# The first pair of blocks: keys first, corner Gram products, and 32x32 turns on VectorE instead of two trips through DRAM

## The chip, the cores and the metric

The kernel runs on one core of a Trainium2 chip. A core has TensorE (PE; its weight loads are listed apart as PEld), VectorE (DVE), ScalarE (ACT), GpSimd (POOL) and SyncE (SP), each with an instruction queue of its own, and 16 DMA engines which the queues of SP, ACT and POOL feed. The metric is device time in microseconds of one execution, the median of several runs.

## The reference

A delta-rule attention over 4 sequences, 8 heads, 768 steps and heads of 48, followed by a two-layer network with a leaky ReLU (384 to 2048 to 384), all in float32.

```python
k_n = k / (np.linalg.norm(k, axis=-1, keepdims=True) + 1e-06)
for t in range(S):
    y[:, :, t] = einsum('bhd,bhde->bhe', q[:, :, t], state)
    v_old = einsum('bhde,bhd->bhe', state, kt)
    state = state + bt * einsum('bhd,bhe->bhde', kt, vt - v_old)
h = x @ w_in          # x: the y of all heads side by side
return np.maximum(0.01 * h, h) @ w_out
```

## The kernel before

The 768 steps are cut into 12 blocks of 64. Within a block the recurrence is solved in closed form: the Gram matrix of the block's keys, scaled by beta over the squared norm, gives a triangular 64x64 system for each of the 32 pairs of head and sequence, and its inverse T turns the loop into matrix products.

Each block passes through these steps, written as Python generators that a function `weave` interleaves in program order; the scheduler of the language then orders every engine's queue by its own estimate of time. `issue_after` (the helper `behind`) pins an instruction behind another one on its engine.

- `gram(n)`, L181: for each of two groups `g` (two sequences each) it loads keys and queries side by side (`kq`, L190), multiplies the keys with keys and queries in one product of 128 columns (`pg`, L207), copies the key half (`gs`, L211), stores its two 32x32 diagonal corners to DRAM (`gd`, L215), masks the query half with the strict triangle (`rq`, L222), keeps the lower-left corner (`gm`, L226), and at last loads the corners back as `L` (L230), one pair of head, sequence and half on each partition.
- `norms` (L237) takes the diagonal of `L`, makes the square root by a bit shift and two Newton steps on VectorE (L245 to L254), and the factor beta over the norm squared.
- `inv(b)`, L278: 31 elimination steps on VectorE (`eliminate`, L269 and L274) turn `L` into the inverse `T` of every 32x32 corner. Blocks 0 and 1 are handled together on 128 partitions, every later block alone on 128 partitions with half the width. The result leaves through DRAM: `td` (L314) and, after a transposing copy `Tt` on ACT (L306), `tt` (L315).
- `merge`, L319: loads `T` into the tile `t` (L325) and its transposed twin into `gm` (L327), both with the rows where TensorE wants them, and makes the lower-left corner of the full inverse with two sets of 32x32 products, `pz` (L341) and `pu` (L349); their copies `zs` (L343) and `rt` (L353, L355) are shared between ACT and VectorE.
- `solve(n)`, L361: loads keys, values and queries (L373, L374), scales the values (`rv`, L395), and makes `pk`, `pw`, `pc`, `py` (L390 to L421); `columns` (L442) transposes the result into the network's input (`px`, split into two parts `xh` and `xl`).
- `ffn(n)`, L455: for each of 16 slices `f` of the hidden width the first layer `ph` (L475), the activation on ACT (L479, L480), the rest `gl` on VectorE (L482), and two slices later the second layer `po` (L465). Weights come as float64 words that are decoded on the chip.
- `weights()`, L134: for each `f` the decoding, one ACT pass (L153) and four VectorE passes (L155, L159, L160, L161), then `low`, which makes the low part of both matrices with TensorE (`wl`, L142 to L144) and ACT (L145, L163). Three slices (KA) are decoded in the prologue; passes of the others are pinned behind the last elimination step of the first pair (`mark["inverse"]`). A weight load (L128) that starts late is gated by a two-column VectorE fill (L126).

The prologue runs gram(0) and gram(1) with three weights, the first inverse, and solve(0). Then, in each block's FFN, the solve of the next block, the inverse of the one after it and the Gram products of the third one ahead are woven in; in block 0's FFN also the remaining weights.

Of the kernel before, what the change touches and what calls it, by code (L numbers as in the profile page):

```python
# [9 lines left out]
F32 = mybir.dt.float32  # L10
# [39 lines left out]
def delta_moe_kernel(ctx: ExitStack, tc, kqT, kv, qT, beta, cst, w_all, out, nblk):  # L50
# [43 lines left out]

    def statics():
        nc.scalar.dma_start(csb, cst)
        for t in ring["t"]:
            nc.vector.memset(t, 0.0)
        for x in "vq":
            for t in ring[x]:  # L100
                nc.gpsimd.memset(t[0:R0], 0.0)

    def identities():
        for t in ring["k"]:
            nc.vector.tensor_copy(
# [15 lines left out]
    def load_w(f, gate=None):  # L121
        if f < NFC:
# [4 lines left out]
            with behind("L"):  # L127
# [6 lines left out]
    def weights():  # L134
# [12 lines left out]
        last = None  # L147
# [28 lines left out]
    def dq(n):  # L176

        return nc.scalar if n < 2 else nc.sync


    def gram(n):  # L181
        if n * NGR >= Q_BUFS:
            need(sv, solve, n - Q_BUFS // NGR)
        kqs = []
        for g in range(NGR):
            t = sb.tile([P, GS, NPAIR, 2, C], F32, tag="kq", name=f"kq{n}_{g}", bufs=KQ_BUFS)
            kqs.append(t)
            with behind("L"):
                for b in range(2):
                    (nc.sync, nc.scalar)[b if n < 2 else 0].dma_start(  # L190
                        t[b * R0:b * R0 + D].rearrange("p s u x t -> p (s u x t)"), kqT[n, g, b])
        b0, i = where[n]
        if i == 0:
            Lh[b0] = sb.tile([P, HC, HC], F32, tag="L", name=f"L{b0}", bufs=2)
        gd = dr.tile([64, HC, HC], F32, tag="gd", name=f"gd{n}")
        for g in range(NGR):
# [4 lines left out]
            ps = [(ps_o if n == 1 else ps_a).tile([P, 512], F32, tag=f"o{b}" if n == 1 else "a", name=f"pg{n}_{g}_{b}") for b in range(2)]  # L201
# [10 lines left out]
            for c in range(2):  # L212
                for e in range(2):
                    a = e * HS + g * GH + c * GU
                    (nc.sync, nc.scalar)[e if n < 2 else 0].dma_start(  # L215
# [12 lines left out]
            if g == NGR - 1:  # L228
                for r in (i,) if len(NB[b0]) > 1 else (0, 1):
                    d = nc.sync.dma_start(Lh[b0][r * 64:(r + 1) * 64].rearrange("l j i -> l (j i)"), gd.rearrange("l j i -> l (j i)"))  # L230
                if n == 1:
                    mark["L"] = d.ins
# [4 lines left out]
    def norms(n, n2):  # L237

        p, w = P, HC
        s, r, c, z = (sb.tile([P, wd], F32, tag=t, name=f"{t}{n}", bufs=b)  # L240
                      for t, wd, b in (("sr", HC, 1), ("rc", HC, 1), ("cb", HC, 2), ("sq", C, 2)))
        nrm[n] = z
        dq(2 * n).dma_start(c, beta[n])
# [15 lines left out]
    def eliminate(b, L, j, T, m):  # L259
# [13 lines left out]
        for tv, t in parts:  # L273
            i = nc.vector.tensor_tensor(t, t, tv, ALU.subtract)  # L274
        if b == 0:
            mark["inverse"] = i.ins

    def inv(b):  # L278

        for n in NB[b]:  # L280
            need(gg, gram, n)
# [4 lines left out]
        with behind("gl"):  # L286
# [319 lines left out]
```

## Time and profile before

| | us |
|---|---|
| median of 3 runs | 711.48 (709.86 to 712.53) |
| the profiled execution's own time | 711.66 |
| its span, first to last instruction | 709.9 |
| TensorE busy | 642.5 |
| VectorE busy | 465.2 |
| ScalarE busy | 332.5 |
| first FFN matmul (`ph`) starts | 93.80 |
| block 0's results are copied out (`ob`) | 174.5 |

The page gives, for each engine, the time it was busy and that share of the span, and cuts the span into 40 slices of some 17.7 us with the busy tenths of each engine in them. In a timeline row the first number is the start, the second the length; the bracket tells how long the engine had been idle before and what ended that. In the chain of waits each row is a piece of the one chain that ended last. Matmul ends are modelled, so starts are the surer numbers there.

### The profile page before, as it was taken

To read this page: it belongs to the slowest core of one execution; us is meant where nothing else is said; L and a number is where in the kernel's file an instruction comes from. 1 tells how busy PE (TensorE), PEld (TensorE's weight loads), DVE (VectorE), ACT (ScalarE), POOL (GpSimd) and SP (SyncE) were. 2 spreads that over 40 slices of the span, in tenths; PEclk is the share of its full clock that TensorE was granted. 3 is DMA by queue.
4 is the path that set the end of the run, shared out by engine and by line. 5 is a ranking of instruction groups with operands and counts; after the bars stand their busy time and mean duration, and the time that the engine had idled before them with its cause. 6 is when DMAs were issued, how large, how long until landed. Compare 5 with 4: busy or idle time off the path is not lost.

```text
span 709.9 us, 21034 instructions
## 1 busy us (share of the span) xinstructions
PE 642.5 (91%) x8424; PEld 591.8 (83%) x8424; DVE 465.2 (66%) x2053; ACT 332.5 (47%) x832; POOL 7.3 (1%) x12
## 2 busy tenths in 40 slices
PE   4800499999999999999999999999999999999996
PEld 3500487889999999999999999999999999999996
DVE  6589159995875975965956947858759759431221
ACT  3311364765463554554544544634635544545422
POOL 4000000000000000000000000000000000000000
PEclk9955599999999999999999999999999999999999
DMA  9295567105527137055065073172270340310001
GB/s 239 40 294 156 110 173 214 48 3 96 130 51 147 31 64 160 4 93 132 3 117 111 2 141 86 39 135 54 52 158 19 66 115 2 69 23 2 13 12 23
DMA packets 128481, 60.90 MB, mean 86 GB/s; under 512 B 115136, under 2 KB 118336, under 8 KB 128384
## 3 DMA queue, kind: packets, MB, share of 16 engines
q1 hardware_dynamic: 115072, 56.81, 35.4%
q10 hardware_dynamic: 13312, 2.76, 2.2%
q8 instruction: 66, 1.08, 0.7%
q14 instruction: 31, 0.25, 0.1%
HBM read 46.96 MB, written 12.58 MB: 84 GB/s over the span
## 4 chain that ended last, share of the span: by engine, by line
PE 81%; DVE 9%; DMA 5%; ACT 2%; issue 1%; ACTq 0%; SPq 0%; DVEq 0%
PE ph L475 29%; PE po L465 27%; PE pw L403 4%; PE pg L207 3%; PE py L421 3%; PE pk L390 3%; DVE rv L395 3%; PE wl L142 3%; PE pc L411 2%; PE pu L349 2%; PE px L450 2%; PE pz L341 2%; DVE tmp L269 1%; DVE T L274 1%; DMA cb<-in_beta 1%
## 5 line engine op out<-in xcount | busy, mean ns | idle before, releaser
L475 PE MATMUL ph<-xh,w 128*128 128x256 f32 x1152 | 248.2, 289 | 0.2 <-DVE gl L482 0.2
L475 PEld LDWEIGHTS ph<-xh,w 128*128 128x128 f32 x1152 | 190.8, 189 | 7.7 <-DVE gl L482 2.1
L465 PE MATMUL po<-w,gh 128*128 128x384 f32 x768 | 190.3, 340 | 2.7 <-ACT gh L479 2.7
L482 DVE TENSOR_TENSOR gl<-ph,gh 128x256 fp32r<-128x256 f32 x192 | 81.2, 424 | 138.5 <-ACT ph L480 128.9
L475 PE MATMUL ph<-xl,w 128*128 128x256 f32 x576 | 166.0, 289 | 0.9
L479 ACT ACTIVATE gh<-ph 128x256 fp32r<-128x256 f32 x192 | 73.9, 385 | 149.4 <-PE ph L475 147.2
L465 PEld LDWEIGHTS po<-w,gh 128*128 128x128 f32 x768 | 131.1, 189 | 4.6 <-ACT gh L479 4.5
L465 PE MATMUL po<-w,gl 128*128 128x384 f32 x384 | 119.5, 340 | 0.0
L274 DVE TENSOR_TENSOR T<-T,tmp 128x60 f32<-128x60 f32 (+35 forms) x661 | 113.0, 208 | 1.2
L269 DVE TENSOR_TENSOR tmp<-T,L 128x60 f32<-128x60 f32 (+35 forms) x661 | 113.0, 208 | 0.7
L475 PEld LDWEIGHTS ph<-xl,w 128*128 128x128 f32 x576 | 108.7, 189 | 4.2 <-DVE xl L119 2.7
L480 ACT ACTIVATE ph<-ph 128x256 f32<-128x256 f32 x192 | 73.4, 382 | 0.0
L465 PEld LDWEIGHTS po<-w,gl 128*128 128x128 f32 x384 | 68.1, 189 | 0.5
L222 DVE TENSOR_TENSOR rq<-pg,csb 64x256 f32<-64x256 f32 x96 | 40.6, 423 | 22.9 <-ACT gs L211 21.8
L341 PE MATMUL pz<-rt,gm 32*32 32x32 f32 x768 | 20.0, 196 | 38.6 <-DMA rt<-td 38.6
L341 PEld LDWEIGHTS pz<-rt,gm 32*32 32x32 f32 x768 | 16.1, 111 | 41.4 <-DMA rt<-td 38.7
L207 PE MATMUL pg<-kq 48*64 48x128 f32 x768 | 35.6, 295 | 5.7 <-DMA kq<-in_kqT 5.7
L207 PEld LDWEIGHTS pg<-kq 48*64 48x64 f32 x768 | 28.3, 144 | 14.7 <-DMA kq<-in_kqT 6.5
L119 DVE TENSOR_TENSOR xl<-px,xh 128x256 fp32r<-128x256 f32 x36 | 14.2, 422 | 29.5 <-ACT xh L118 29.1
L392 ACT ACTIVATE rt<-pk 48x512 f32<-48x512 f32 x44 | 26.1, 593 | 13.2 <-PE pk L390 12.4
L142 PE MATMUL wl<-cg,csb 128*128 128x384 f32 x64 | 28.3, 538 | 4.2 <-ACT gs L211 4.2
L405 ACT COPY rv<-pw 64x384 f32<-64x384 f32 x48 | 22.7, 472 | 18.1 <-PE pw L403 17.3
(67 smaller groups left out, 665.4 us busy)
## 6 DMA issues: line engine op xcount, KB each, us to landing
wr<-in_w_all SPq DMA_DIRECT2D x16, 768.0 KB, 6.7
kq<-in_kqT SPq DMA_DIRECT2D x44, 192.0 KB, 4.2
L<-gd SPq DMA_DIRECT2D x22, 256.0 KB, 3.8
rk<-in_kv SPq DMA_DIRECT2D x24, 192.0 KB, 3.2
rv<-in_kv SPq DMA_DIRECT2D x24, 192.0 KB, 4.2
rq<-in_qT SPq DMA_DIRECT2D x24, 192.0 KB, 3.9
out<-ob SPq DMA_DIRECT2D x48, 96.0 KB, 3.0
gd<-gs SPq DMA_DIRECT2D x88, 32.0 KB, 2.7
```

The lines of the kernel that those rows point to most:

```text
L142: nc.tensor.matmul(d, eye, g[:, cols], start=True, stop=False)
L207: nc.tensor.matmul(ps[b][c * 64:(c + 1) * 64, p * 128:(p + 1) * 128], kq[r, c ^ b, p, 0], kq[r, c ^ b, p].rearrange("p x t -> p (x t)"), s ...
L222: nc.vector.tensor_tensor(qa[DN, c, b * NPAIR:(b + 1) * NPAIR], pv[b][r, 1], tri[r].rearrange("p (o t) -> p o t", o=1).broadcast_to([C, NP ...
L269: nc.vector.tensor_tensor(tv, t[:, :, j:j + 1].broadcast_to([P, k, w]), L[:, j, j + 1:].rearrange("p (o w) -> p o w", o=1).broadcast_to([P ...
L274: i = nc.vector.tensor_tensor(t, t, tv, ALU.subtract)
L341: nc.tensor.matmul(zv[h * 64:h * 64 + HC, u], gt[lo, l], t[lo, h, u, HC:], start=True, stop=True)
L403: nc.tensor.matmul(pv[r, u], t[:, c, u], v[:, c, u], start=True, stop=True)
L465: i = nc.tensor.matmul(po[t][:, :DO], a[:, ts_], w[f], start=(f == 0 and k == 0), stop=(f == NFC - 1 and k == 2))
L475: nc.tensor.matmul(ph, a[f][:, cc * P:(cc + 1) * P], x[cc][e], start=(k == 0), stop=(k == 3 * NCC - 1))
L479: nc.scalar.activation(gh, ph, AF.Prelu, alpha=0.01)
L480: i = nc.scalar.activation(ph, ph, AF.Prelu, alpha=0.01)
L482: i = nc.vector.tensor_tensor(gl, ph, gh.bitcast(F32), ALU.subtract)
```

## The change

Only the first pair of blocks (0 and 1) and the prologue are rewritten; blocks 2 to 11 keep their way through DRAM.

- The keys and queries of blocks 0 and 1 come in a layout of their own (`kq0`): four key loads first, on SP's and ACT's queue, then constants and beta, then four query loads. Everything else on SP (weights, the first k, v, q) is pinned behind the last of them.
- `first()` makes the two 32x32 diagonal corners of each Gram matrix directly as 32x32 products, placed in PSUM so that two copies and one VectorE transpose of 32x32 blocks on 128 partitions give `L`. Then come the lower-left corners (`low`) and the key-query products (`bank`); the masks are pinned behind the inverse.
- After the elimination two VectorE transposes of T make `Tc` and `Gc`; `merge` copies rows of `Tc` into `t` with ACT and VectorE and multiplies with `Gc` directly. For these two blocks `zs` and `rt` are all ACT's.
- KA goes from 3 to 1 and WEARLY from 7 to 8: one weight is decoded ahead of the inverse, eight are loaded at the start. The fills of `t` and `T` and the identities move from VectorE to GpSimd. The scaling of block 0's values is pinned behind the inverse.
- The new tiles lie in the slots of late weights: keys in 12 and 13, queries in 10 and 11, the copied corners in 9, `Gc` and `Tc` in 14 and 15.

The core of the diff:

```diff
+        fill(0, kx, (nc.sync, nc.scalar))
+        nc.scalar.dma_start(csb, cst)
+        c = nrm["c"] = sb.tile([P, HC], F32, tag="cb", name="cb0", bufs=2)
+        nc.scalar.dma_start(c, beta[0])
+        mark["kq"] = fill(1, qx, (nc.scalar, nc.sync)).ins
...
+        for g in range(NGR):
+            for i, y, u, (k, _) in each(g):
+                l = (g * GU + u) * HC
+                for e in range(2):
+                    h = k[:, e * HC:(e + 1) * HC]
+                    nc.tensor.matmul(diag[y][i * 64 + e * HC:i * 64 + (e + 1) * HC, l:l + HC], h, h, start=True, stop=True)
+        for y in range(2):
+            (nc.scalar.copy, nc.vector.tensor_copy)[y](S[:, y], diag[y])
+        nc.vector.transpose(L, S.rearrange("p y (l t) -> p t (y l)", t=HC))
+        yield
+        for g in range(NGR):
+            for i, y, u, (k, _) in each(g):
+                nc.tensor.matmul(low[y][corner[i], l:l + HC], k[:, HC:], k[:, 0:HC], start=True, stop=True)
+            for n in range(2):
+                    nc.scalar.copy(m[R0 + HC:P, y].rearrange("p u t -> p (u t)"), low[y][corner[n], g * GU * HC:(g + 1) * GU * HC])
...
+                nc.tensor.matmul(bank[g][y][i * 64:(i + 1) * 64, u * C:(u + 1) * C], k, q, start=True, stop=True)
...
+                    with behind("inverse"):
+                        nc.vector.tensor_tensor(
+                          of("q", n, g)[DN, :, y * NPAIR:(y + 1) * NPAIR], bank[g][y][r].rearrange("p (c u t) -> p c u t", c=2, u=NPAIR),
...
-                Tt = sb.tile([P, HC * HC], F32, tag="L", name=f"Tt{b}", bufs=2) if two else X[:, M * HC:]
+                if two:
+                    Tc, Gc = early("tc", (15, 14), (HS, HC))
+                    nc.vector.transpose(Tc.rearrange("p l i -> p i l"), T.rearrange("p m i -> p i m"))
+                    d = nc.vector.transpose(Gc.rearrange("p l m -> p m l"), T)
+                    mark["inverse"] = d.ins
...
+            if n < 2:
+                a = n * 64 + e * HC
+                (nc.scalar.copy if e or n else nc.vector.tensor_copy)(
+                    d, T[a:a + HC].rearrange("p (y g u) i -> p g y u i", y=2, g=NGR)[:, g])
...
-            (nc.scalar.copy, nc.vector.tensor_copy)[h](zs[r1, h], zv[h * 64:h * 64 + HC])
+            (nc.vector.tensor_copy if h and n > 1 else nc.scalar.copy)(zs[r1, h], zv[h * 64:h * 64 + HC])
...
+                with behind("inverse" if not n else None):
...
-    weave(2, (gg, NGR, 0, 2))
-    for k in range(KA):
-        load_w(k)
-    weave(2, (gg, NGR, 0, 2))
+    for f in range(KA):
+        load_w(f)
+    for g in range(NGR):
+        fetch(0, g)
+    for f in range(KA, WEARLY):
+        load_w(f)
     signs()
     weave(1, (wg, KA, 0, 1))
-    identities()
     weave(1, (iv, NI, 0, 1))
+    next(fg)
+    next(fg)
     weave(1, (sv, NS, 0, 1))
...
-WAHEAD, WEARLY = 4, 7
-KA, WB = 3, 12
+WAHEAD, WEARLY = 4, 8
+KA, WB = 1, 12
```

More of the change, by code (lines that the diff above doesn't have):

```diff
@@ L187, in gram @@
             kqs.append(t)
-            with behind("L"):
+            with behind("kq"):
                 for b in range(2):
[L190 to L194, printed above, removed]
+                    nc.sync.dma_start(t[b * R0:b * R0 + D].rearrange("p s u x t -> p (s u x t)"), kqT[n, g, b])
+        b0 = where[n][0]
+        Lh[b0] = sb.tile([P, HC, HC], F32, tag="L", name=f"L{b0}", bufs=2)
         gd = dr.tile([64, HC, HC], F32, tag="gd", name=f"gd{n}")
@@ L228, in gram @@
             if g == NGR - 1:
[L229 to L232, printed above, removed]
+                for r in range(2):
+                    nc.sync.dma_start(Lh[b0][r * 64:(r + 1) * 64].rearrange("l j i -> l (j i)"), gd.rearrange("l j i -> l (j i)"))
                 done.add((gram, n))
@@ L285, in inv @@
         T = X[:, 0:M * HC].rearrange("p (m i) -> p m i", m=M)
-        with behind("gl"):
-            nc.vector.memset(T, 0.0)
+        if two:
+            nc.gpsimd.memset(T, 0.0)
+        else:
+            with behind("gl"):
+                nc.vector.memset(T, 0.0)
         yield
@@ L366, in solve @@
         nt = sb.tile([P, NGR, 2, GU], F32, tag="nt", name=f"nt{n}", bufs=2)
-        nc.scalar.copy(nt[DN].rearrange("p g h u -> p (g h u)"), ps[DN, 0:HS])
-        def load(g):
-            merge(n, g, of("t", n, g))
-            with behind("L"):
-                for i, x in enumerate("kv"):
-                    nc.sync.dma_start(of(x, n, g)[DN].rearrange("p h u t -> p (h u t)"), kv[n, g, i])
-                nc.sync.dma_start(of("q", n, g)[UP].rearrange("p h u t -> p (h u t)"), qT[n, g])
+        if n < 2:
+            for y in range(2):
+                nc.scalar.copy(nt[DN, :, :, y * NPAIR:(y + 1) * NPAIR],
+                               ps[DN, y * GH:(y + 1) * GH].rearrange("p (g h v) -> p g h v", g=NGR, h=2))
+        else:
+            nc.scalar.copy(nt[DN].rearrange("p g h u -> p (g h u)"), ps[DN, 0:HS])
+        def load(g):
+            merge(n, g, tv(n, g))
+            if n:
+                fetch(n, g)
         def heads(rows):
@@ L384, in kt @@
         def kt(g):
[L386 removed]
+            t, k, v = tv(n, g), of("k", n, g), of("v", n, g)
             if n:
@@ L516, in delta_moe_kernel @@
     wg = weights()
-    gg = chain(gram, range(nblk))
+    fg, gg = first(), chain(gram, range(2, nblk))
     iv = chain(inv, range(len(NB)))
@@ L565, in _layout @@
     bt = bt.reshape(nblk, 64, HC)
-    bts = np.stack([np.concatenate([bt[0], bt[1]])] + [np.concatenate([bt[n], bt[n]]) for n in range(2, nblk)])
+    b0 = bt[0:2].reshape(2, 2, NGR, 2, 2, NPAIR, HC).transpose(0, 1, 4, 2, 3, 5, 6).reshape(P, HC)
+    bts = np.stack([b0] + [np.concatenate([bt[n], bt[n]]) for n in range(2, nblk)])
     cst = np.zeros((P, NCST), np.float32)
```

162 lines of the change are left out of this document (108 added, 54 removed).

## Prediction

> **What bounds the kernel now.** I read the page first, then one table of busy time by stage, then the chain of waits for the first 100 us, then single rows of the timeline. From the page: the span, each engine's share, and TensorE's busy tenths in 40 slices.
>
> ```profile
> span 709.9 us, 21034 instructions
> PE 642.5 (91%) x8424; PEld 591.8 (83%) x8424; DVE 465.2 (66%) x2053; ACT 332.5 (47%) x832; POOL 7.3 (1%) x12
> PE   4800499999999999999999999999999999999996
> ```
>
> From the sixth slice on TensorE is full and nothing but TensorE sets the end. The holes are in the first five slices. The stage table (cut where the chain changes hands) puts numbers on that; its columns are the length, then the busy time of PE, PEld, DVE, ACT and POOL, the granted clock, the DMA share and GB/s.
>
> ```profile
> 0.00:37.66 37.66, 23.51 (x152) 16.39 (x152) 22.77 (x41) 12.21 (x23) 7.35 (x12) 0.97 0.58 144
> 37.66:66.33 28.67, 0.42 (x2) 0.29 (x2) 28.15 (x149) 3.41 (x6) 0.00 (x0) 0.50 0.75 201
> 66.33:79.65 13.32, 0.00 (x1) 0.00 (x1) 6.13 (x8) 4.33 (x4) 0.00 (x0) 0.50 0.95 259
> 79.65:93.87 14.22, 13.62 (x329) 12.88 (x329) 2.11 (x5) 5.30 (x13) 0.00 (x0) 0.63 0.29 59
> 93.87:174.50 80.63, 79.08 (x873) 68.00 (x874) 68.34 (x236) 51.46 (x116) 0.00 (x0) 1.00 0.42 108
> 174.50:709.90 535.40, 525.88 (x7071) 494.20 (x7069) 337.73 (x1616) 255.76 (x672) 0.00 (x0) 1.00 0.33 69
> ```
>
> Six stages: Gram products and the first bounce through DRAM (37.66 us); norms and elimination, all VectorE (28.67); the second bounce, TensorE idle (13.32); block 0's solve up to the first FFN matmul (14.22, TensorE busy but at a clock of 0.63); block 0's FFN, where TensorE is busy 79.08 of 80.63 and VectorE 68.34; and all the rest. The chain of waits says what ends each early stage:
>
> ```profile
> 33.90 3.71 DMA L<-gd
> ...
> 37.70 0.20 DVE sr L245
> ...
> 42.33 1.98 DVE rv L395 x4
> ...
> 64.22 0.41 issue
> ...
> 66.14 0.19 DVE T L274
> ...
> 66.35 0.32 ACT Tt L306
> ...
> 67.66 7.15 DMA td<-T
> ...
> 76.22 3.38 DMA rt<-td
> ...
> 79.65 1.09 PE pz L341 x32
> ```
>
> The reader is to see two DRAM trips on the chain, and two places where VectorE, the only worker of the second stage, does something else: 1.98 us of rv products and, from 64.22 to 66.14, weight decoding ahead of the last elimination step.
>
> **The change, part by part.** I date each event of the new prologue from the start of the span, then put the unchanged stages behind it. These timeline rows price the pieces:
>
> ```profile
> 4.11 1.97 PE L207 MATMUL pg<-kq 48*64 48x128 f32 x16 [4.11 <-DMA kq<-in_kqT]
> 79.65 1.07 PE L341 MATMUL pz<-rt,gm 32*32 32x32 f32 x32 [38.56 <-DMA rt<-td]
> 84.15 3.65 PE L403 MATMUL pw<-rv,rt 128*64 128x48 f32 x64
> 115.76 0.69 PE L341 MATMUL pz<-rt,gm 32*32 32x32 f32 x32
> 1.02 0.91 DVE L98 MEMSET rt<- 128x1024 f32 x1 [1.02 <-PEq L596]
> 41.01 1.28 DVE L299 TENSOR_TENSOR L<-L,cb 128x512 f32<-128x512 f32 x2
> 66.35 2.03 ACT L306 COPY Tt<-T 128x1024 f32<-128x1024 f32 x1 [15.95 <-DVE T L274]
> 80.76 0.36 ACT L343 COPY zs<-pz 32x256 f32<-32x256 f32 x1 [3.65 <-PE pz L341]
> 81.16 0.42 DVE L343 COPY zs<-pz 32x256 f32<-32x256 f32 x1 [8.70 <-ACT zs L343]
> 82.95 0.37 ACT L355 ACTIVATE rt<-pu 32x256 f32<-32x256 f32 x1 [0.30 <-PE pu L349]
> ```
>
> *A, until L stands.* Keys now come before queries and weights. The first 192 KB load is used at 4.11; the four key loads are of that size on the same two queues, so group 0 starts there too. The diagonal corners are 128 products, 256 instructions as the trace counts (768 pg instructions for 384 products). The nearest row is pz, 32 columns at the cold clock: 1.07/32 = 33 ns, so 8.4 us. Above it stands pw, 3.65/64 = 57 ns (14.6 us); below, pz again, in block 0 at the full clock, 0.69/32 = 22 ns (5.5 us). I take 33 ns because its shape is the same: 4.1 + 8.4 = 12.5.
> The Trainium skill, "TensorEngine Tiling (Array Packing)", Instruction Overhead, speaks against the cut: a matmul costs about 60 cycles however short it is; at the throttled 1.2 GHz that the skill's "TensorE: Matmul & The Clock Gate", What's actually happening, gives, that is an estimate of 50 ns, 12.8 us here and 4.4 us more in the sum. The row of 33 ns disagrees, and the measurement decides.
> Then one copy of 512 columns out of PSUM on ACT and DVE side by side (twice the 0.36 of ACT's 256 columns is 0.7), and the turn of 1024 columns. The trace has no turn. It lies between 0.91 (a plain fill of 128x1024) and 2.03 (ACT's strided copy of that shape); I take 1.28, VectorE's own two passes over 512 columns. L stands at 14.5 with the gaps.
> The Trainium skill, "VectorE: DVE Perf Modes", The three transpose paths, gives 311 ns for a turn of 128x128 in 32x32 blocks, in bf16; eight of these, an estimate of 2.5 us per turn, would make the sum 2.4 us more. No run here shows it.
>
> *B, weight 0.* Before, three weights are decoded in this stretch; now one, and its four passes have no rule that keeps them out of the way of the norms. The group rows of block 0 and the loads' rows:
>
> ```profile
> L161 DVE SCALAR_TENSOR_TENSOR cg<-wr,cg 128x768 uint32<-128x768 uint32 x10 | 9.5, 954 | 0.1
> L160 DVE SCALAR_TENSOR_TENSOR cg<-wr,cg 128x768 uint32<-128x768 uint32 x10 | 9.5, 950 | 0.1
> L159 DVE TENSOR_SCALAR cg<-cg 128x768 uint32<-128x768 uint32 x10 | 5.6, 557 | 0.1
> L155 DVE TENSOR_SCALAR cg<-cg 128x768 f32<-128x768 f32 x10 | 5.6, 555 | 1.8 <-ACT cg L153 1.7
> 10.23 0.90 ACT L153 ACTIVATE cg<-wr 128x768 f32<-128x768 f32 x1 [3.73 <-DMA wr<-in_w_all]
> 14.67 0.89 ACT L153 ACTIVATE cg<-wr 128x768 f32<-128x768 f32 x1 [0.43 <-DMA wr<-in_w_all]
> 10.00:20.00 10.00, 5.19 (x34) 3.65 (x34) 8.52 (x18) 4.32 (x7) 0.00 (x0) 1.00 0.86 233
> wr<-in_w_all SPq DMA_DIRECT2D x3, 768.0 KB, 10.1
> ```
>
> One decoding is 0.95 + 0.95 + 0.56 + 0.56 = 3.02 us. Ahead of w0 in the queues lie eight loads of 192 KB, the constants and beta, with w0 about 2.4 MB; at 233 GB/s that is 10.5 us, so it lands near 13, just when L stands. I charge the whole 3.0 (bounds 0, if it slips behind, and 5, if VectorE also stands waiting for it): norms start at 17.5.
>
> *C, norms and elimination.* 37.70 to 66.33 is 28.6 us. The rv products go behind the inverse (-2.0), and so does all later decoding (64.22 to 66.14, of which one 0.17 us step remains: -1.75). 24.9 us are left, T is done at 42.4. Nothing else shortens it: the 31 steps are the same.
>
> *D, the second bounce.* Tt, six stores, twelve loads and their waits go (and before the norms sixteen gd stores and two L loads). In their place: one turn (1.28; the second one is needed only by pu), then ACT's copy of T's rows into t (0.36): pz starts at 44.1 instead of 79.65.
>
> *E, to the first FFN matmul.* 14.22 us as before: TensorE will have idled some 20 us, so the clock, 0.50 in both idle stages, is again what it was. For the first two blocks both zs halves and both rt halves go to ACT one after the other: 0.36 + 0.37 twice, +1.5 at most as they now follow each other in both groups. First ph at 59.8 (was 93.87).
>
> *F, block 0.* Two more weights are expanded here (13 lows before, 15 now). One half of one, from the chain, and the last decoding pass of the stage, from the timeline:
>
> ```profile
> 95.22 0.65 PE wl L142 x2
> 95.87 0.17 PE wl L143
> 96.04 0.17 PE wl L144
> ```
>
> ```profile
> 148.36 0.96 DVE L161 SCALAR_TENSOR_TENSOR cg<-wr,cg 128x768 uint32<-128x768 uint32 x1
> ```
>
> That is 2 x 0.99 us per weight, +4.0 on TensorE, which has 1.5 us of slack. VectorE: ten decodings fell into this stage, so six were done at its start. Now one, plus what fits between T and ph: 17.4 us less two turns (2.6), rv (2.0), masks (eight of 512 columns at 0.64, 5.1) and copies (about 1) leave 6.7 us, two weights. Three decodings (9.1 us) move into the stage, and four zs and rt passes of 0.42 leave it. VectorE is then at 68.3 + 9.1 - 1.7 = 75.7 of some 85 us, still under TensorE, but crowded in its first two thirds; I add 2.0 for waits there. Block 0: 80.6 + 4.0 + 2.0 = 86.6, ending at 146.4.
>
> *G.* 535.4 us unchanged: span 681.8. The profiled run took 711.66 with a span of 709.9, so 1.8 lie around it: **683.6 us**. The median of the runs is 711.48, 0.2 below the profiled one, which I leave out.
>
> *Charged at nothing.* The fills of t and T and the identities move to GpSimd, hidden by 17 us without a user (all twelve fills of before took it 7.3 us, and five more passes of that kind make it some 13; if late, the diagonal copy of T waits). The corner copies (eight on ACT) and the k-q products run in the 25 us of elimination. Masks come behind the inverse and in front of py, under 9 us of pz, pu and pw; without that cover, four of them are 2.6 us. On SP's queue block 0's k, v, q and eight weights are issued at once, not after the bounce; earlier for all. One new wait: loading weights 14 and 15 needs the slots of the two turned tiles, so a small VectorE fill waits for block 1's merge, and decodings, elimination and gl queue behind it. Weight 10, which triggers it, comes about four FFN steps after that merge, some 20 us; without them the step would pay a landing of 10.1 us.
>
> **The rivals.**
> *VectorE becomes block 0's bound.* If nothing but weight 0 is decoded by the first ph, five decodings (15.1) move in, and block 0's last decoding, done at 149.3 before, comes 15.1 - 1.7 + 2.6 (second masks) = 16 us later in the stage. If TensorE's 25 us behind it stay, block 0 takes 96.6 and the time is 693.6. For it: VectorE's 68.34 us lie mostly ahead of 149.3. Against: the 25 us themselves, a backlog of TensorE that can shrink.
> *The fine Gram cut is dear*, at pw's 57 ns: +6.2, 689.8. For: it alternates row groups as pz does not. Against: it spreads over eight places of the array (two row halves, four column groups) where pw has two.
> *The early part is better than charged*: weight 0 lands late enough to slip behind (-3), the products at 22 ns (-2.9), ACT's extra passes hidden (-1.5), no waits in block 0 (-2): 674.2.
> *Weight 0 takes the bounce's place*, the one that ends slower. Its passes stand in VectorE's queue ahead of the norms, and its load shares the engines with everything now issued at once: 9.2 MB with all eight weights and block 0's k, v, q. At the 233 GB/s of the row it lands at 39.5, the norms start at 42.5, and it costs 25 us more; from a landing at about 42 on the whole gain is gone, and at the 144 GB/s of the first stage (64 us) the norms start at 67 and it ends at 733. Against it: the three weights issued together before were used at 10.23 and up to 14.67, in order, so a queue serves its loads one after another.
> *Nothing of it reaches the end*, because another early wait holds the FFN: no row shows one, since DMA is at 0.58 of its time in the first stage.
>
> **How the numbers follow.** Forecast 0.52 (676 to 688); VectorE-bound block 0 0.20 (689 to 697); dear Gram cut 0.08 (688 to 692); better early part 0.13 (668 to 676); weight 0 holds 0.05, half of that slower; no change 0.02. The range 668 to 697 leaves out the last two and the tails, about 0.15. Half a per cent, 3.6 us, is about what a measurement of this kernel can tell from no change; every case but the last two is beyond it: faster 0.94, same 0.03, slower 0.03.
>
> **What would show it.** Right: no gd, td or tt traffic for the first pair; L's turn ending near 14.5 and lasting 1 to 2 us; one uninterrupted run of elimination steps of 20 us; pz at 44, first ph at 60, the end of block 0 at 146, and from there 535 us. Wrong: pz after 55 (A to C mis-sized; look for VectorE waiting on a weight load), a clock of 1.00 in stage E, or TensorE idle by more than 5 us in block 0.

## The result, and the profile after

The changed kernel takes 693.12 us (median of 4 runs, 692.78 to 694.39) against 712.0 us for the kernel before (median of 4, 709.86 to 713.48): a ratio of 0.974, 95% interval 0.9711 to 0.9769, so it is faster by 2.3 to 2.9%. The forecast was 683.6 us with a range of 668 to 697. The gain is there and inside the range; it is two thirds of the size forecast, 18.9 us of 28.

The page of the changed kernel, its span, TensorE's row and TensorE's busy tenths in 40 slices:

```profile
span 691.6 us, 21757 instructions
...
PE 639.5 (92%) x8808; PEld 590.2 (85%) x8808; DVE 459.4 (66%) x2029; ACT 337.0 (49%) x848; POOL 10.7 (2%) x17
...
PE   2416999999999999999999999999999999999996
```

TensorE is full from the fifth slice on, and not from the sixth. The stage table, cut at the same events as that of before (L stands; the elimination is done; first pz; first FFN product ph; end of block 0), has the same columns: length, busy time of PE, PEld, DVE, ACT and POOL, granted clock, DMA share, GB/s.

```profile
0.00:21.10 21.10, 7.58 (x298) 5.49 (x298) 5.57 (x7) 4.00 (x6) 10.72 (x17) 1.00 0.95 232
21.10:45.93 24.83, 5.95 (x225) 4.91 (x224) 24.32 (x137) 6.73 (x17) 0.00 (x0) 0.66 0.78 240
45.93:48.65 2.72, 0.00 (x0) 0.00 (x0) 2.69 (x2) 0.67 (x2) 0.00 (x0) 0.50 0.00 0
48.65:71.50 22.85, 16.07 (x333) 14.67 (x333) 17.27 (x28) 12.54 (x26) 0.00 (x0) 0.61 0.08 21
71.50:156.60 85.10, 83.70 (x894) 70.80 (x893) 72.58 (x244) 58.42 (x130) 0.00 (x0) 1.00 0.49 130
156.60:691.60 535.00, 526.15 (x7064) 494.32 (x7062) 336.96 (x1614) 254.64 (x670) 0.00 (x0) 1.00 0.32 67
```

Row against row: the first stage fell from 37.66 to 21.10 us, the elimination from 28.67 to 24.83, the second bounce from 13.32 to 2.72. From there on time was given back: the stage up to the first FFN product grew from 14.22 to 22.85, block 0's FFN from 80.63 to 85.10. The rest is as it was. Three early stages won 31.0 us, two later ones returned 13.1.

Against the forecast, in span (681.8 forecast, 691.6 measured): norms start 3.6 us late, the turn and copy take 1.0 more, the solve of block 0 takes 7.1 more, block 0's FFN 1.5 less, the rest 0.4 less: +9.8. Rows of the timeline (start, duration, engine, line, what, and in brackets the idle time ahead of it with what ended it) show where. TensorE first:

```profile
4.15 3.43 PE L218 MATMUL ph<-kx 48*32 48x32 f32 x223 [4.15 <-DMA kx<-in_kq]
13.77 0.47 PE L218 MATMUL ph<-kx 48*32 48x32 f32 x33 [6.20 <-issue]
...
57.43 3.66 PE L500 MATMUL pw<-rv,rt 128*64 128x48 f32 x64 [2.88 <-DVE rt L410]
...
66.20 0.88 PE L547 MATMUL px<-csb,ys 128*128 128x128 f32 x4 [2.15 <-ACT ys L520]
```

The first two rows are the corner products. Their PSUM tile is called `ph` like the FFN's first layer, and the trace counts two instructions for each product, 256 in all. They run at 15 ns each (3.43 us for 223); then TensorE stands, that is, it is idle, for 6.20 us before the last 33, with no data to wait for that the trace shows. The norms did not wait for this stop. The chain of waits goes another way:

```profile
0.74 3.70 DMA kx<-in_kq
...
4.46 9.87 DMA wr<-in_w_all
...
14.35 0.91 ACT cg L157
...
15.28 0.57 DVE cg L159
```

Weight 0's decoding lies ahead of the corner copy in VectorE's queue. It began at 15.28 us, when the weight had landed and ScalarE had made its first pass, and its last pass ended at 18.43; the corner products had ended at 14.24. Later TensorE stands twice in block 0's solve: for VectorE's copy of T (L410), and for ScalarE's copy of the attention output (ys). VectorE over the same time:

```profile
17.47 0.96 DVE L165 SCALAR_TENSOR_TENSOR cg<-wr,cg 128x768 uint32<-128x768 uint32 x1
18.34 0.68 DVE L220 COPY S<-ph 128x512 f32<-128x512 f32 x1
19.13 1.93 DVE L221 STREAM_TRANSPOSE L<-S 128x1024 f32<-128x1024 f32 x1
21.10 0.19 DVE L311 TENSOR_SCALAR sr<-L 128x32 uint32<-128x32 uint32 x1
...
47.78 1.88 DVE L374 STREAM_TRANSPOSE tc<-T 128x1024 f32<-128x1024 f32 x1
49.69 1.28 DVE L242 TENSOR_TENSOR rq<-pq,csb 64x512 f32<-64x512 f32 x2
50.90 1.27 DVE L242 TENSOR_TENSOR rq<-ph,csb 64x512 f32<-64x512 f32 x2
52.20 1.97 DVE L492 TENSOR_TENSOR rv<-rv,nt 64x384 f32<-64x384 f32 x4
54.20 1.30 DVE L242 TENSOR_TENSOR rq<-pq,csb 64x512 f32<-64x512 f32 x2
55.42 1.30 DVE L242 TENSOR_TENSOR rq<-ph,csb 64x512 f32<-64x512 f32 x2
56.75 0.75 DVE L410 COPY rt<-tc 32x512 f32<-32x512 f32 x2
57.54 1.50 DVE L159 TENSOR_SCALAR cg<-cg 128x768 f32<-128x768 f32 x3
```

All eight masks (L242, blocks 0 and 1) and the scalings (L492) stand in the queue ahead of the short copy L410 for which pw waits; block 1's masks, 2.6 us, aren't wanted until much later. ScalarE does the like to ys:

```profile
60.41 1.25 ACT L410 COPY rt<-tc 32x512 f32<-32x512 f32 x2
61.69 0.97 ACT L502 COPY rv<-pw 64x384 f32<-64x384 f32 x2
62.68 1.25 ACT L410 COPY rt<-tc 32x512 f32<-32x512 f32 x2
63.96 1.69 ACT L167 CAST w<-cg 128x768 fp32r<-128x768 f32 x2
65.67 0.48 ACT L520 COPY ys<-py 128x384 f32<-128x384 f32 x1
```

Both L410 rows are block 1's copies of T, 2.5 us, and the two casts are those of weights 1 and 2 (weight 3's follows, ahead of the second ys). None of it is needed for the first FFN product, and ys is.

### The profile page after: what moved, and what is told of

The parts are those of the page before. It is cut to its first block, busy times and chain, and to the rows that moved or that the text cites. A ratio compares the mean times of both kernels' runs of the same rounds, so it can differ in the third digit from the quotient of the medians.

```text
span 691.6 us, 21757 instructions
## 1 busy us (share of the span) xinstructions
PE 639.5 (92%) x8808; PEld 590.2 (85%) x8808; DVE 459.4 (66%) x2029; ACT 337.0 (49%) x848; POOL 10.7 (2%) x17
## 4 chain that ended last, share of the span: by engine, by line
PE 83%; DVE 10%; DMA 3%; ACT 2%; issue 1%; SPq 1%; ACTq 0%; DVEq 0%
PE ph L572 30%; PE po L562 28%; PE pw L500 3%; PE pk L486 3%; PE py L518 3%; PE wl L146 3%; PE pg L271 3%; PE pc L508 3%; DVE rv L492 3%; PE pu L435 2%; PE px L547 2%; PE pz L427 2%; DVE T L340 1%; DVE tmp L335 1%; DMA wr<-in_w_all 1%
## 5 line engine op out<-in xcount | busy, mean ns | idle before, releaser
L286 DVE TENSOR_TENSOR rq<-pg,csb 64x256 f32<-64x256 f32 x80 | 33.8, 423 | 15.2 <-ACT gs L275 14.2
L427 PE MATMUL pz<-rt,gm 32*32 32x32 f32 x768 | 20.3, 196 | 17.9 <-ACT rt L410 17.9
L492 DVE TENSOR_TENSOR rv<-rv,nt 64x384 f32<-64x384 f32 x48 | 23.7, 555 | 9.6 <-ACT nt L465 9.6
L500 PEld LDWEIGHTS pw<-rv,rt 128*64 128x64 f32 x768 | 24.9, 145 | 5.7 <-issue 3.0
```

What stands on the lines that cost most here:

```text
L286: nc.vector.tensor_tensor(qa[DN, c, b * NPAIR:(b + 1) * NPAIR], pv[b][r, 1], tri[r].rearrange("p (o t) -> p o t", o=1).broadcast_to([C, NP ...
L427: nc.tensor.matmul(zv[h * 64:h * 64 + HC, u], gt[lo, head(h, u)], t[lo, h, u // NPAIR, u % NPAIR, HC:], start=True, stop=True)
L492: nc.vector.tensor_tensor(v[DN, :, us], v[DN, :, us], nt[DN, g, :, us].rearrange("p h (u o) -> p h u o", o=1).broadcast_to([C, 2, NPAIR, D ...
L500: nc.tensor.matmul(pv[r, u], t[:, c, u // NPAIR, u % NPAIR], v[:, c, u], start=True, stop=True)
```

## The experiments

Theory at the start: the missing 7 us of the solve are queue order, and putting block 0's own work first on VectorE and ScalarE brings the first ph, and with it the end, forward. Rival: block 0's FFN is held by something else, so an earlier first ph is given back there. Each kernel is the changed kernel with the edit shown.

**VectorE's order.** Block 1's masks and the decodings of weights 1 and later go behind VectorE's two copies of T for block 0.

```diff
-            with behind("inverse" if f >= KA else None):
+            with behind("copy" if f >= KA else None):
...
-                    with behind("inverse"):
+                    with behind("copy" if n else "inverse"):
...
+                if not (e or n):
+                    mark["copy"] = i.ins
```

> Changed kernel with one order pinned: block 1's masks and the decodings of weights 1 and later come behind the two copies of T's upper rows (32x512) on VectorE. Queue theory: these copies then end at 55.0 instead of 57.5, pw starts 2.4 us earlier; but ys waits on ACT behind the casts of weights 1 to 3, which wait for decodings that end no earlier, so the next wait is just as late and the total moves by 0 to -1 us (692 to 693). Rival (the stretch from pz to the first ph is bound by TensorE at its half clock): no change in pw's start beyond 1 us and no change in the total.

Measured: 699.34 us (698.03 to 701.5), ratio to before 0.9796 (0.9761 to 0.9831): slower than the changed kernel, all four of whose runs lie below all four of these. pw started at 55.7 us and not at 57.4, but the first ph stayed at 71.5 (the wait for ys took what was won), and block 0's FFN grew to 93.3 us. The largest piece of that lies in the middle of the FFN, and was no part of the theory. Its VectorE row there:

```profile
100.07 0.19 DVE L311 TENSOR_SCALAR sr<-L 128x32 uint32<-128x32 uint32 x1 [5.33 <-DMA L<-gd]
```

and its TensorE row:

```profile
104.73 0.58 PE L574 MATMUL ph<-xh,w 128*128 128x256 f32 x1 [5.14 <-DVE gl L581]
```

This sr is the first step of block 2's norms. Block 2 still sends its Gram matrices through DRAM; VectorE stands 5.33 us for them, the residual gl of the FFN is queued behind, and TensorE stands 5.14 us for that; its busy time in block 0 grows as well, from 83.70 to 87.01 us, at a mean clock of 0.96. In the changed kernel VectorE's stand at that row is 0.90 us. The order on VectorE is set ahead of time from a simulated timing, so a small edit changes what lies ahead of that wait.

**ScalarE's order**, and **both orders**. The casts of weights 1 to 4 and block 1's copies of T go behind the splits of block 0's columns.

```diff
-            nc.scalar.copy(t[:, 0:2 * DO], g)
+            with tc.issue_after(mark["x"][2]) if 0 < f < 5 else nullcontext():
+                nc.scalar.copy(t[:, 0:2 * DO], g)
...
+                with tc.issue_after(mark["x"][2]) if n == 1 else nullcontext():
+                  (nc.scalar.copy if e or n else nc.vector.tensor_copy)(
```

> Changed kernel with one order pinned on ACT: the casts of weights 1 to 4 and block 1's copies of T's rows come behind the three xh casts of block 0. Queue theory: ys follows py at once (1.6 us earlier), xh follows px (some 1.5 us more), first ph at 68 instead of 71.5, total 690 (688.5 to 691.5). Rival (TensorE at its half clock is the bound): under 1 us.

> Both orders pinned. Queue theory: the two gains add, since each removes the wait that follows the other: first ph at 65.5 to 66.5, total 687 (686 to 689). The stretch from pz to ph falls from 22.9 to about 17.5 us. Rival (half clock): 692 to 693, the stretch stays at 22.

Measured: 693.89 us (0.9725, 0.9695 to 0.9755) with ScalarE's order alone, 696.35 us (0.9748, 0.9711 to 0.9785) with both. The intervals don't part them from the changed kernel; the events do. (Three of the four runs with both orders took 696.1 to 696.7 us and one 692.72; the trace is of one of the three.) The first ph came at 67.1 and 66.1 us and not at 71.5, as the theory of queue order has it. But block 0 ended at 158.0 and 159.9 us and not at 156.6. What was won ahead of the FFN was lost in it. Windows of the kernel with both orders:

```profile
66.14:159.90 93.76, 89.41 (x898) 74.36 (x897) 72.56 (x244) 63.98 (x138) 0.00 (x0) 0.95 0.45 119
96.00:100.00 4.00, 2.02 (x71) 1.91 (x72) 2.27 (x6) 0.90 (x3) 0.00 (x0) 1.00 0.80 249
100.00:104.00 4.00, 3.68 (x10) 2.27 (x10) 3.63 (x14) 2.25 (x6) 0.00 (x0) 0.50 0.00 0
104.00:108.00 4.00, 4.00 (x37) 2.51 (x36) 2.64 (x11) 2.17 (x5) 0.00 (x0) 0.50 0.22 33
108.00:112.00 4.00, 4.00 (x17) 3.12 (x16) 1.37 (x5) 2.34 (x5) 0.00 (x0) 0.72 0.42 167
```

```profile
98.94 0.39 PE L577 MATMUL ph<-xh,w 128*128 128x256 f32 x1 [1.98 <-DVE gl L584]
```

TensorE stands 1.98 us for gl behind block 2's norms, and from 100 us on its clock is 0.50 for some 10 us. Its busy time in block 0 is 89.41 us where the changed kernel needs 83.70 for nearly the same products (898 and 894 instructions): 5.7 us, most of the 8.7 by which block 0 got longer. The other long stand, 2.05 us at 74.27, is the price of the new order itself: TensorE waits for gh, the first activation of the FFN, in front of which ScalarE now makes the casts and copies that were pushed back.

**The rest of the early part.** Three kernels: weight 0 decoded behind the inverse, its load still first; three weights decoded ahead of it; weights 1 to 7 and block 0's loads held until the corners are copied.

```diff
-KA, WB = 1, 12
+KA, WB = 0, 12
...
-    weave(1, (wg, KA, 0, 1))
...
     weave(1, (sv, NS, 0, 1))
+    weave(1, (wg, 1, 0, 1))
```

```diff
-KA, WB = 1, 12
+KA, WB = 3, 12
```

```diff
+            i = (nc.scalar.copy, nc.vector.tensor_copy)[y](S[:, y], diag[y])
+        mark["S"] = i.ins
...
+    for f in range(KA, WEARLY):
+        load_w(f, "S")
     for g in range(NGR):
         fetch(0, g)
-    for f in range(KA, WEARLY):
-        load_w(f)
```

> Changed kernel with weight 0, too, decoded behind the inverse (KA = 0, its load as early as before); nothing else. Theory that weight 0 in VectorE's queue holds the norms: the corner copy runs at 14.3 instead of 18.3, the norms start at 17 instead of 21.1, pz comes 4 us earlier at 44.6. Its decoding (3.0 us), cast and low part then stand between pz and the first ph, so of these 4 us between 0 and 2 are left: total 691 to 694. Rival (the early part is held by TensorE's pause from 7.5 to 13.8 and not by weight 0): norms start within 1 us of 21.

> Changed kernel with three weights decoded ahead of the inverse (KA = 3 as before the change). Head-start theory: the two decodings cost the norms and the elimination 6 us and more if VectorE waits for their loads, and give back 4.0 us of TensorE in block 0's FFN and some waiting there: total 693 to 698. Rival (VectorE's late start on the weights is what bounds block 0's FFN): faster than 691.

> Changed kernel whose weights 1 to 7 and block 0's k, v, q are loaded only after the corner copy on VectorE (each weight's load waits for a two-column fill behind that copy); keys, queries and weight 0 as before. Theory that the crowd of early loads delays both TensorE's next instructions (its pause of 6.2 us from 7.5 on waits for nothing in the data) and weight 0's landing (14.3): the pause shrinks to under 3 us, weight 0 lands by 12, the norms start 2 to 4 us earlier, total 689 to 691. Rival (the pause belongs to the products themselves): same pause, norms at 21, total 693 or more, as the weights come later.

Measured: weight 0 behind, 699.51 us (0.9803, 0.9775 to 0.9832); three first, 696.93 us (0.9756, 0.9711 to 0.98); loads later, 693.04 us (0.9709, 0.9665 to 0.9753). With weight 0 behind, the norms start at 17.85 us instead of 21.10 and the first ph comes at 67.6, 3.9 us earlier, yet block 0 takes 95.2 us. Its VectorE row shows the largest piece:

```profile
98.87 0.19 DVE L311 TENSOR_SCALAR sr<-L 128x32 uint32<-128x32 uint32 x1 [6.00 <-DMA L<-gd]
```

TensorE waited 6.13 us behind it, and its clock was 0.50 from 100 to 108 us. With three weights first, the first ph comes at 77.3 us and block 0 takes 82.3: two decodings less in it save 2.8 us of 85.1, although TensorE stands 2.43 us there for gl, and cost 5.8 ahead of it. Holding the loads back moved the norms by 0.6 us only, as weight 0 landed 0.6 earlier (13.71 us). It also tells that the other loads are not what stops TensorE among the corner products, for the stop is there without them, 5.86 us where it was 6.20 (the DMA rate over the first stage is 132 GB/s and not 232):

```profile
13.52 0.47 PE L220 MATMUL ph<-kx 48*32 48x32 f32 x33 [5.86 <-issue]
```

**What each turn is worth.** T through DRAM instead of by the two turns; the corners through DRAM instead of by L's turn, with the loads of block 0 and of weights 1 to 7 behind that trip, as before the change.

```diff
-                    nc.vector.transpose(Tc.rearrange("p l i -> p i l"), T.rearrange("p m i -> p i m"))
-                    d = nc.vector.transpose(Gc.rearrange("p l m -> p m l"), T)
+                    nc.scalar.copy(Tt.rearrange("p i m -> p m i"), T)
...
+                        nc.scalar.dma_start(td[q].rearrange("m l i -> l m i"), T[r])
+                        nc.scalar.dma_start(Tc[r].rearrange("p l i -> p (l i)"), td[q].rearrange("m l i -> m (l i)"))
```

```diff
-        nc.vector.transpose(L, S.rearrange("p y (l t) -> p t (y l)", t=HC))
+            nc.scalar.dma_start(gd[q].rearrange("l j t -> j l t"), S[r].rearrange("p y (l t) -> p (y l) t", t=HC))
+        mark["L"] = nc.sync.dma_start(L.rearrange("p j t -> p (j t)"), gd.rearrange("q l j t -> (q l) (j t)")).ins
```

> Changed kernel with only the second trip restored: T goes through DRAM (four stores and four loads of 128 KB, a strided ACT copy and two stores and two loads for its turned twin) into the same tiles, in place of the two VectorE turns. Theory: from T's end to pz takes 13 us as before the change instead of 2.7, of which VectorE's freed 4 us and earlier masks give back 2 to 3 at pw: total 700 to 704. Rival (the second trip was hidden behind the masks and scaling anyway): 694 to 697.

> Changed kernel with only the first trip restored: the copied corners go through DRAM (four stores of 128 KB on ACT's queue, one load of 512 KB on SP's) in place of L's turn; as before the change, the other loads stay behind that load. Theory: the trip takes some 7 us against 1.9, and the fewer loads in flight give back up to 3 through an earlier weight 0: total 695 to 699. Rival (keys first and the small products are the whole gain of the first part, the trip itself is cheap without traffic): 692 to 694.

Measured: 711.03 us with the second trip back (0.9975, 0.995 to 0.9999), 703.38 us with the first one back (0.9843, 0.9785 to 0.9901; its four runs spread from 698.43 to 705.92, and the trace is of the longest). With the first trip back the norms start at 30.25 us, 9.2 later, and that arrives at the end: first ph +10.4, block 0's end +12.1, median +10.3. The chain of waits of that kernel has the trip in two pieces:

```profile
20.58 3.61 DMA gd<-S
24.27 5.96 DMA L<-gd
```

With the second trip back the first ph is 9.8 us later and the median 17.9. Here the price is not the trip's alone. Ahead of it, on VectorE, masks, scalings and three clamps (45.43 to 54.31 us in the chain) came to stand in front of the last elimination step. Behind it, block 2's norms stood 5.49 us for their own trip, and block 0 took 92.9 us. From T's end to pz it is 8.1 us (54.42 to 62.56) where the changed kernel needs 2.72. So both trips lie on the path. Bringing them back costs 10.4 and 9.8 us at the first ph, where the change had won 22.4; but the second figure holds a changed order on VectorE too, and the price of that trip alone is not shown.

**Is it block 2's trip that holds block 0?** Two ways to take VectorE's stand away, on the changed kernel and on the one with both orders. First, block 2's inverse is woven into the FFN from step 7, its Gram products left at step 2.

```diff
-        weave(NF, (ff, NF, 0, NF), (wg, NFC * (n == 0), 0, WB), (sv, NS * (n + 1 < nblk), 2, 11),
-              (iv, NI * (n + 2 < nblk), 2, NF), (gg, NGR * (n + 3 < nblk), 11, 13))
+        weave(NF, (ff, NF, 0, NF), (wg, NFC * (n == 0), 0, WB), (sv, NS * (n + 1 < nblk), 2, 11), (gg, NGR * (n == 0), 2, 3),
+              (iv, NI * (n + 2 < nblk), 2 if n else 7, NF), (gg, NGR * (n + 3 < nblk), 11, 13))
```

> The changed kernel with one edit: block 2's inverse (its norms on VectorE, which wait for block 2's Gram matrices to come back from DRAM) is woven into block 0's FFN from step 7 and not from step 2; its Gram products stay at step 2. Theory (block 0 is held by VectorE standing in the norms of block 2, with residuals and decodings queued behind): here that stand is short already (TensorE waits 0.8 us behind it), so the end of block 0 goes from 156.6 to 154.5-156.5 and the time is 690.5-693. Rival (the twelve decodings on VectorE set the pace, in whatever order): no change, 692.5-694. Either way, if the later inverse makes block 1 wait, a stretch after 157 us gets longer and the time is above 694.

> Both orders of e3 (block 0's VectorE and ScalarE work ahead of block 1's) with block 2's inverse woven in from step 7. Theory (the norms' stand on VectorE ate e3's gain of 5.4 us at the first ph): first ph stays at about 66, TensorE's waits for gl and gh behind the norms (4 us in e3) go, the clock in 96 to 116 us stays above 0.95 (0.70 and 0.79 in e3), block 0 takes 83-86 us and ends at 149-152, and the time is 685.5-689.5. Rival (decodings on VectorE, or their gated loads, set block 0's end): block 0 ends at 157-160 as in e3, with the waits moved to another gl, and the time is 692.5-696.5.

Second, with both orders, block 2's loads and stores of that trip go to GpSimd's queue.

```diff
-                    nc.sync.dma_start(
-                        gd[a:a + GU].rearrange("l j i -> j l i"),
+                    (nc.sync if n > 2 else nc.gpsimd).dma_start(
+                        gd[a:a + GU].rearrange("l j i -> j l i"),
```

> Both orders of e3, and block 2's own trip (its key and query loads, its four Gram stores of each group and the two loads of L) issued from GpSimd's queue and not from SyncE's, where they stand behind weight loads that wait for VectorE's decodings. Theory (the trip is late because of its place in SyncE's queue): the norms of block 2 start at 90-95 us and not at 98.4, TensorE's waits of 4 us behind them go, block 0 ends at 149-153 and the time is 685.5-690. Rival (the trip is late because the Gram products and copies are, or because GpSimd's DMAs are no faster): norms at 97-100, block 0 ends at 157-160, the time is 692.5-697.

Measured: 693.26 us for late norms alone (0.9719, 0.9677 to 0.976), 693.89 us with both orders (0.9732, 0.9684 to 0.978), 694.31 us with GpSimd's queue (0.9732, 0.9691 to 0.9772). Late norms alone change nothing: block 0 ends at 156.8 us, the rival's figure, where the theory had 154.5 to 156.5. With both orders and late norms the stand behind the norms is gone, the clock is 1.00 all through block 0, and block 0 ends at 155.9 us, 4.0 earlier than with both orders alone: this part of the theory holds. The stand for gh was never behind the norms, and it stays:

```profile
74.83 0.96 PE L567 MATMUL po<-w,gh 128*128 128x384 f32 x4 [2.06 <-ACT gh L581]
```

An end at 149 to 152 was expected, and against the changed kernel only 0.7 us are left of an FFN that starts 4.8 us sooner; in the medians (693.89 against 693.12) nothing is left. GpSimd's queue gave the same end (156.0) for another reason than expected: block 2's norms started not earlier but at 101.24 us, after 1.65 us of waiting for the trip, and a gl had come to stand ahead of them in VectorE's queue.

Two stands of VectorE are left, in the kernel with both orders and late norms:

```profile
74.54 0.56 DVE L160 TENSOR_SCALAR cg<-cg 128x768 f32<-128x768 f32 x1 [5.27 <-ACT cg L158]
...
103.08 0.56 DVE L160 TENSOR_SCALAR cg<-cg 128x768 f32<-128x768 f32 x1 [4.86 <-ACT cg L158]
```

and in these of its ScalarE:

```profile
68.78 2.31 ACT L169 CAST w<-cg 128x768 fp32r<-128x768 f32 x3
71.10 2.50 ACT L413 COPY rt<-tc 32x512 f32<-32x512 f32 x4
73.63 0.88 ACT L158 ACTIVATE cg<-wr 128x768 f32<-128x768 f32 x1
...
102.13 0.91 ACT L158 ACTIVATE cg<-wr 128x768 f32<-128x768 f32 x1 [0.17 <-PE wl L147]
```

The first row is weight 4's decoding, the first of twelve that fall into the FFN. In the changed kernel it starts at 75.48 us, here at 74.54, with both orders alone at 73.97: the work that was pushed off ys's way, 4.8 us of casts and copies, now stands right ahead of weight 4's first step on ScalarE, and of the gh that TensorE waits for. Moving work along one full queue does not remove it. The second pair is a ring: a decoding needs one of three cg buffers, TensorE frees one when it has built the low half (wl), and TensorE is in block 1's merge just then. VectorE stands 4.86 us there, where the changed kernel's VectorE does block 2's norms. TensorE itself stands in block 0 for gh (2.1 us), for zs (0.9) and for gl (1.0 in two waits), so the work ahead of gh costs it more than the ring does. That the date of weight 4's decoding sets block 0's end is a theory so far.

**Taking that work off ScalarE.** VectorE's order and late norms, with block 1's copies of T and the casts of weights 1 to 3 on GpSimd, which is idle. ScalarE's order is not in this kernel, so weight 4's cast is no longer pinned either.

```diff
-            nc.scalar.copy(t[:, 0:2 * DO], g)
+            (nc.gpsimd.tensor_copy if 0 < f < 4 else nc.scalar.copy)(t[:, 0:2 * DO], g)
...
-                (nc.scalar.copy if e or n else nc.vector.tensor_copy)(
+                i = (nc.gpsimd.tensor_copy if n else nc.scalar.copy if e else nc.vector.tensor_copy)(
```

> e10 with two kinds of work moved from ScalarE to GpSimd, which stands idle there: block 1's four copies of the inverse (2.50 us on ScalarE in e10, right ahead of weight 4's first step) and the casts of weights 1 to 3 (2.31 us). Theory (block 0's end hangs on when weight 4's decoding starts, 74.5 us in e10 and 75.5 in the changed kernel, and comes some 81 us after it in both): weight 4's first VectorE step starts at 70-72 us, block 0 ends at 151.5-153.5 and the time is 689-691.5. Rival 1 (TensorE's own work sets the end from the start of the weights' later decodings on, or VectorE loses as much again between weights 7 and 9): weight 4 is earlier by as much but block 0 ends at 155-157, and the time is 693-695. Rival 2 (GpSimd's copies are slow, or slow VectorE down): VectorE's steps in 50 to 70 us get longer, weight 4 starts at 74 or later, the time is 693-697.

Measured: 691.8 us (690.75 to 692.68, 5 runs), ratio 0.9713 (0.9685 to 0.9741), span 689.3. Weight 4 starts at 72.48 us, a little later than expected, and block 0 ends at 154.6: 1.3 us better than both orders with late norms for 2.1 us of earlier decoding, between the theory and rival 1. The stand of 2.06 us for gh is gone in the same stroke, so the run does not tell which of the two gave the 1.3 us. GpSimd's rows cost more than ScalarE's did:

```profile
58.47 1.58 POOL L410 COPY rt<-tc 32x512 f32<-32x512 f32 x2 [47.22 <-PE pw L502]
60.65 1.63 POOL L410 COPY rt<-tc 32x512 f32<-32x512 f32 x2 [0.60 <-PE pw L502]
65.82 3.70 POOL L167 CAST w<-cg 128x768 fp32r<-128x768 f32 x3 [3.54 <-issue]
```

It is the lowest median of all these kernels, but its interval overlaps that of the changed kernel, and 1.3 us between two medians is less than 0.5%: a better kernel is not shown.

The two windows of block 0 that sum this up, of the kernel with both orders and late norms, and of this last one:

```profile
66.69:155.93 89.24, 85.29 (x898) 71.48 (x897) 73.23 (x246) 63.88 (x137) 0.00 (x0) 1.00 0.48 132
```

```profile
66.50:154.61 88.11, 84.65 (x898) 71.93 (x897) 75.06 (x249) 59.07 (x130) 3.02 (x3) 1.00 0.50 135
```

The changed kernel is busy 83.70 of 85.10 us there. With both orders and late norms TensorE starts 4.8 us earlier, stands 3.95 us instead of 1.40 (2.1 of it for gh) and is busy 1.6 longer at the same clock (0.4 of it for four px products that came before the first ph in the changed kernel): 4.1 of the 4.8 us are gone.

## Why the prediction was right, and where it was wrong

The measured 693.1 us lie inside the stated range of 668 to 697, but not in the 676 to 688 of the forecast's own case. They fall among the 689 to 697 that were given to VectorE as block 0's bound, with a chance of 0.20, and that did not happen. So the direction and most of the gain come from the mechanism that was forecast, two trips less on the chain; that the number still fell inside is in part luck. Of the signs of being wrong none appeared (pz at 48.65 us, clock 0.61 in E, TensorE idle 1.40 us in block 0), though the first ph was 11.7 us late.

**A, until L stands: too early, with the order on VectorE the wrong way round.** The first load (4.11 forecast, 4.15 measured) was right. The products, put at 33 ns by pz's row, take 15; a stop of 6.20 us without data to wait for, which no row of before shows, made the last one end at 14.24 instead of 12.5. But neither set the start of the norms. The sum had L first and weight 0's decoding behind it; in the queue the decoding came first and could not begin before 15.28, as weight 0 landed at 14.35 where "near 13" was forecast. With 3.06 us for the decoding and 2.76 for copy and turn, where 3.0 and 2.0 were charged, that makes 21.10 instead of 17.5. The turn was mis-sized: 1.93 us where 1.28 was taken, inside the bounds of 0.91 and 2.03. The Trainium skill's figure in "VectorE: DVE Perf Modes", The three transpose paths, had given an estimate of 2.5; the trace lies between the two. The Trainium skill's rule of 60 cycles in "TensorEngine Tiling (Array Packing)", Instruction Overhead, spoke for dearer products; the row of 15 ns says the opposite for products spread over eight places of the array.

**B, weight 0: right in price.** 3.0 us were charged; without the decoding the norms start 3.25 us earlier. That saving did not reach the end in the run that made it: block 0, with one more decoding in it and TensorE's stand of 6.13 us, took 10.1 us longer.

**C, norms and elimination: right**, 24.83 for 24.9, one uninterrupted run.

**D, the second bounce: right in kind**, 2.72 for 1.7; the turn again, and ScalarE's copy of 512 columns priced by a row of 256. The chains of the two kernels that bring the trips back go through them.

**E, to the first ph: wrong, the step that failed.** "14.22 us as before", and 1.5 more, became 22.85. The granted clock was as forecast on average (0.61 against 0.63). What failed is an item charged at nothing: "Masks come behind the inverse and in front of py, under 9 us of pz, pu and pw; without that cover, four of them are 2.6 us." They did not lie under pw: with the scalings they stood ahead of VectorE's copy of T that pw needs, and block 1's copies of T and two casts, for which the sum has no term, stood ahead of ys on ScalarE. TensorE's two stands for them are 5.03 us (2.88 and 2.15). Its work also got slower behind them: before, its clock was back at 1.00 for the last 3 us ahead of the first ph; here it was 0.69 over the last 5.5, and pc took 255 ns a piece instead of 210. Shown by order: with both queues rearranged the first ph comes at 66.1 us, 5.4 us earlier, of the 7.1.

**F, block 0: right in size** (86.6 forecast, 85.1 measured, VectorE 72.58 busy where 75.7 was forecast, since three weights and not two were decoded between T and the first ph), **wrong in form**. The forecast hung block 0 on the first ph, "ending at 146.4". The runs show that its end does not follow the first ph when that comes earlier: with the first ph at 66.1, 66.7 and 67.6 us block 0 took 93.8, 89.2 and 95.2. When it comes later by the first trip, the end does follow (81.9 us, 86.8 long). So, as far as these runs show, mending step E alone brings little. The eight kernels from 691.8 to 696.4 us, the changed one among them, that start the FFN between 66.1 and 71.5 us end block 0 between 154.6 and 159.9.

**G: right**, 535.0 for 535.4.

**The rivals.** *VectorE becomes block 0's bound* had named 693.6 us and the result is 693.1, yet by another road. Four weights and not one were decoded by the first ph, block 0 took 85.1 us and not 96.6, and the time went in A and E. That the number agrees is chance. Something like its mechanism may hold block 0 once E is mended: a loop over VectorE, ScalarE and TensorE (decoding, cast, low half, free buffer) with block 2's DRAM trip in VectorE's queue. The rows show the waits of that loop; that it sets block 0's end is argued and not shown. *The dear Gram cut* was the wrong way round. *The early part is better than charged* had cheaper products and no waits in block 0; the products came out cheaper still, and it did not matter, as the norms waited for weight 0. *Weight 0 takes the bounce's place* was right in kind, for the chain does go through weight 0's load and decoding, and far off in size: weight 0 was used at 14.35 us, with eight weights in the queues, and holding the others back won 0.6 us on the norms and nothing at the end.

Left open: what stops TensorE for 6 us among the corner products (in the changed kernel the stop is off the chain), what sets block 0's end once E is mended, and whether more cg buffers would free the ring, which was not tried.

## What to carry to other kernels

When a long wait at the head of a kernel goes, reprice the stage behind it by the queues of each engine, in order, and not by its old length: what used to be done during the wait now stands ahead of the first instruction that matters. And before counting an earlier start as gain at the end, ask what else the next stage waits for; here its buffers, its decodings and another block's DRAM trip had dates of their own, and 4.8 us of earlier start were worth 0.7 at the end of block 0.

## What the runs showed of the hardware

- A VectorE turn of 128x1024 f32 in 32x32 blocks takes 1.88 to 1.93 us in the changed kernel, with any of the three patterns used there, and 1.85 to 1.97 over all thirteen kernels.
- Products of 48x32 by 48x32, spread over two row halves and four column groups, go through at 15 ns for each of their two instructions (223 in 3.43 us).
- Among these products TensorE stops for 5.5 to 6.3 us after the 223rd of 256 instructions in all thirteen kernels that have them, also where weight 0 waits and where the other loads are held back. The traces put no data wait to it. With weight 0 behind, two more such stops (2.88 and 2.81 us) follow after exactly 128 and 256 further matmul instructions; in ten others a smaller one (0.24 to 1.42 us) follows after 255. So the place goes with the count of instructions; the cause is not shown.
- In block 0's full FFN the granted clock fell to 0.50 behind stands of TensorE of 1.97 and 1.70 us (ScalarE's order, some 3.4 us at 0.50 behind each), 1.98 us (both orders, some 10 us), 2.43 us (three weights first, some 3.4 us) and two of 0.83 and 0.61 us close together (first trip back, some 3.4 us). It did not fall behind stands of 2.05 and 2.06 us at about 74 us (both orders, without and with late norms), nor behind 0.80 and 0.61 in the changed kernel. The Trainium skill, "TensorE: Matmul & The Clock Gate", What's actually happening, has the clock fall after an idle window of about 3.4 us that runs freely. The stretches at 0.50 agree with that length or three times it, but the stands ahead of them were shorter, so the length of a single wait does not tell which one costs the clock.
- The clock in a profile's row can read 1.00 where the products go at about half pace. Before the change 16 pg products took 1.97 us at 4.11 and 1.09 us at 30.00, both with a clock of 1.00; with weight 0 behind, 32 pz products took 1.06 us at a clock of 1.00, as in the changed kernel at 0.50.
- GpSimd's cast of 128x768 takes 1.23 us where ScalarE's takes 0.77 to 0.84, and its copy of 32x512 0.79 to 0.82 where ScalarE's takes 0.62 (last kernel, and both orders with late norms).
